# An expert's two weights in one transfer, and the queries' left-over rows behind the odd batches' rows

## The chip, the cores and the metric

The kernel runs on one core of one Trainium2 chip. What is counted is the device time of one execution, in microseconds (us). The core has a matrix engine (TensorE, PE in the profile), a vector engine (DVE), a scalar engine (ACT), GpSimd (POOL) and SyncE (SP). SP issues nearly all transfers from memory here and does nothing else; its transfers form one queue that 16 DMA engines work off. A tile has 128 partitions, and one row of a transfer is what goes to one partition.

## The reference

Three stages, all in float32, on 8 batches of 576 tokens (4608 tokens), 8 heads of 64:

```python
# slot attention
a = softmax(phi, over the 576 tokens)            # 32 memory slots per head
k_m, v_m = a^T k, a^T v                          # 32 x 64 per head
x = softmax(q k_m^T / 8, over the slots) v_m     # 4608 x 512
# soft mixture of 8 experts with 4 slots each
logits = x phi                                   # 4608 x 32
slot_input = softmax(logits, over the tokens)^T x        # 8 experts x 4 rows x 512
slot_out[e] = relu(slot_input[e] w1[e]) w2[e]    # w1: 512 x 1024, w2: 1024 x 512
x = softmax(logits, over the slots) slot_out     # 4608 x 512
# MLP
out = softplus(x w_in) w_out                     # 512 -> 2048 -> 512
```

An expert works on four rows only, so its two matrices of 2 MB each are used by few and short matmuls. The experts' weights are 33.6 of the 85.0 MB that the kernel reads.

## The kernel before, in words

**Stages.** The attention goes through the batches in order. Of each batch it loads `phi`, `kv` and `q`; the 576 tokens are 512 and 64 left over, and the left-over rows of two batches are scored together. Then the dispatch softmax gives the experts' inputs, the experts run, and their outputs are folded with the first MLP matrix; the MLP takes the rest.

**Who decides the order.** The program is written by a planner, `Flow` (lines 149 to 275). Each step of the kernel is a generator that yields units: a list of (engine, estimated us) and the tokens and slots that the unit needs. `Flow` starts the unit that can start earliest by these estimates, so the order of instructions on each engine follows from the estimated durations of the loads too. `keep_warm` puts idle matmuls (line 938) where the planner's own times show gaps on PE.

**Loads.** All loads are issued by SP in one order: first `attention_loads` (line 428), which per batch yields kv, the next batch's phi, q, and with an odd batch `qm`, the left-over rows of two batches. Then `weight_loads` (line 1086): four MLP transfers, the experts' weights `w` (`load_w1`, line 1036, and `load_w2`, line 1044) in the order w1 of expert 0, w2 of expert 0, and so on to expert 5, then w1 of 6 and 7, w2 of 6 and 7, and then the other `wi` and `wo` of the MLP. The last w2 comes in parts of 1, 0.5 and 0.5 MB. An instruction on SP that waits holds up those behind it.

**Room.** Each load needs a free slot of a ring or pool. `q` has a ring of 3 slots of 8 KB per partition, `qm` one of 2 slots of 2 KB; a slot is free when the scores (`raw_scores`, line 568, matmul in line 591) that read it are done. The experts' weights have 8 slots of 16 KB (`w16`, line 1013), which lie where the attention had its buffers; a slot is given back in line 1259 after an expert's first layer, or in line 1296 after its second.

**The experts on PE.** `first_layer` (line 1244) computes `hid` with w1 (matmul in line 1251), ACT applies relu (`hs`), PE transposes (`hTp`, line 1267), ACT copies it to `hT`. `second_layer` (line 1275) adds every expert's product of `hT` and w2 into `S` (line 1284). After the last expert's, `slot_out` sums up the parts (`sop`, line 1308). Between them stand transposes `ctp` (line 1221) of the combine weights `c` (line 1215).

Of the kernel before, what the change touches and what calls it, by code (L numbers as in the profile page):

```python
# [134 lines left out]

    "left": 52000,

    "rings": (("kv", 3), ("phi", 3), ("a", 4), ("kt", 6), ("s", 2), ("q", 3), ("qm", 2)),

    "stick": 'm1 n2 n3 r3 t1',  # L140
}
# [7 lines left out]
class Flow:  # L149
# [50 lines left out]
    def free(self, name, i=0):  # L200
        self.pools[name].append((*self.now, i))
# [77 lines left out]
def tile_slot_attention_soft_moe_softplus_mlp(  # L279
    ctx: ExitStack,  # L280
    tc: tile.TileContext,
    q: bass.AP,
    qm: bass.AP,
    kv: bass.AP,
    phi: bass.AP,
    moe_phi: bass.AP,
    moe_w1: bass.AP,
    moe_w2: bass.AP,
    w_in: bass.AP,
    w_out: bass.AP,  # L290
    out: bass.AP,
# [50 lines left out]
    def weight_pools(stack, name, some):  # L342
# [12 lines left out]
    A_ORDER = (2, 3, 0, 1)  # L355
    sizes = {
        "kv": 2 * KV + KVL, "phi": NG * S, "kt": 256, "s": (SC + 1) * 2 * TM, "a": (SC + 1) * 2 * TM,
        "q": 4 * 128 * SC, "qm": 4 * 128,
    }
    for tag, n in PLAN["rings"]:  # L360
        pools = B1 if tag in ("kv", "phi") else BB
# [49 lines left out]
                done(f"kv{b}{g}")  # L411

    def load_q(b):
        yield [("D", 2.52)], ["+q"], 0
        t, held["q", b] = ring("q")
        nc.sync.dma_start(out=t, in_=q[b])
        q_t[b] = t.rearrange("p (k n) -> p k n", k=4)
        done(f"q{b}")
        if b % 2 == 0:
            return  # L420
        pr = b // 2
        yield [("D", 0.63)], ["+qm"], 0
        t, held["qm", pr] = ring("qm")
        nc.sync.dma_start(out=t, in_=qm[pr])
        qm_t[pr] = t.rearrange("p (k b n) -> p k b n", k=4, b=2)
        done(f"qm{pr}")

    def attention_loads():
        yield from load_phi(0)
# [138 lines left out]
    def raw_scores(b, half):  # L568


        pr, bb = divmod(b, 2)
        yield [("P", 0.3 if half else 0.95)], (
            [f"qm{pr}", f"km{b}0", f"km{b}1", f"sr{b}"] if half
            else [f"q{b}", f"km{b}0", f"km{b}1", "+a"]
        ) + ["+raw"]
        if not half:
            a, held["a", b] = ring("a")
            raw_t[b] = a
            a_t[b] = a.rearrange("p (c x) -> p c x", c=SC + 1)
# [19 lines left out]
        if half:  # L599
            free("qm", held["qm", pr])  # L600
        else:
            free("q", held["q", b])
# [407 lines left out]
    pp = px.enter_context(tc.tile_pool(name="pp", bufs=1, reuse_waits="tile", space=PSUM))  # L1010
    ex = px.enter_context(tc.tile_pool(name="ex", bufs=1, reuse_waits="tile"))
    w8.update(weight_pools(ctx, "w8", range(NWS, NW1)))
    w16 = weight_pools(px, "w16", range(NW1 // 2, (NW8 + NWX) // 2))
    vacant = [
        max([t for x, y, t in taken if x < edge - 8192 * i and y > edge - 8192 * (i + 1)], default=0.0)
        for i in range(NW8 + NWX)
    ]
    flow.pools["w8"] = [(vacant[i], "", i) for i in w8]
    flow.pools["w16"] = [(max(vacant[2 * i : 2 * i + 2]), "", i) for i in w16]

    def slot8(shape, dtype, name, i=None):

# [5 lines left out]

    w1_t, w2_t, raw_t, at = {}, {}, {}, {}

    def slot16():

        i = flow.got["w16"]
        return i, w16[i].tile([128, 4096], F32, tag="w16", name="w16")

    def load_w1(e):
        yield [("D", 4.93)], ["+w16"], 0
        at["w1", e], t = slot16()
        nc.sync.dma_start(out=t, in_=moe_w1[e])
        for n in range(2):  # L1040
            w1_t[e, n] = t[:, 2048 * n : 2048 * n + 2048].rearrange("p (k f) -> p k f", k=KC)
        done(f"w1{e}")

    def load_w2(e):
        last = e == NE - 1
        parts = ((0, 2048), (2048, 3072), (3072, 4096)) if last else ((0, 4096),)
        for a, b in parts:
            yield [("D", 4.93 * (b - a) / 4096)], [] if a else ["+w16"], 0
            if a == 0:
                at["w2", e], t = slot16()  # L1050
                for n in range(2):
                    w2_t[e, n] = t[:, 2048 * n : 2048 * n + 2048].rearrange("p (h k d) -> p h k d", h=2, k=4)
            nc.sync.dma_start(out=t[:, a:b], in_=moe_w2[e][:, a:b])
            for n in range(2):
                for half in range(2):
                    if a <= 2048 * n + 1024 * half < b:
                        done(f"w2{e}{n}.{half}")
# [28 lines left out]
    def weight_loads():  # L1086
        early = list(EARLY)
        for _ in range(early_at.count(-1)):
            x = early.pop(0)
            yield from load_wi(x[1]) if x[0] == "wi" else load_wo(x[1])  # L1090
        for e in range(NE):
            for x in (e, e + 1) if e == NE - 2 else (e,) if e < NE - 2 else ():
                yield from load_w1(x)
            yield from load_w2(e)
            for _ in range(early_at.count(e)):
                x = early.pop(0)
                yield from load_wi(x[1]) if x[0] == "wi" else load_wo(x[1])
# [146 lines left out]
    def first_layer(e):  # L1244
        yield [("P", 2.0)], ["SX", f"w1{e}", "+hid"]
        if e == NE - 1:
            flow.product = product
        hid = pp.tile([128, 256], F32, tag="hid", bufs=2, name="hid")
        for kc in range(KC):
            for j in range(4):  # L1250
                nc.tensor.matmul(  # L1251
                    hid[32 * j : 32 * j + 32],
                    lhsT=SX[:, kc, NS * e : NS * e + NS],
                    rhs=w1_t[e, j // 2][:, kc, 256 * (j % 2) : 256 * (j % 2) + 256],
                    start=(kc == 0),
                    stop=(kc == KC - 1),
                    skip_group_check=True,
                )
        free("w16", at["w1", e])
        yield [("A", 0.39)], []  # L1260
        hs = ex.tile([128, 256], F32, tag="hs", bufs=2, name="hs")
        nc.scalar.activation(hs, hid, AF.Relu)
        free("hid")
        yield [("P", 0.22)], ["+hTp"]
        hTp = pp.tile([128, 2, 128], F32, tag="hT", name="hTp")
        for cb in range(2):
            nc.tensor.transpose(hTp[:, cb], hs[:, 128 * cb : 128 * cb + 128], ident)
        yield [("A", 0.39)], ["+hT"]
        hT = ex.tile([128, 2, 4, NS], F32, tag="hTs", bufs=2, name="hT")
        nc.scalar.activation(hT.rearrange("p c j s -> p c (j s)"), hTp, AF.Copy)  # L1270
        free("hTp")
        hT_t[e] = hT
        done(f"hT{e}")

    def second_layer():
        for n in range(2 * NE):
# [16 lines left out]
                    done(f"s2{half}")  # L1293
                    flow.add(slot_out(half), -1e5 + half, "ex")
            if kb:
                free("w16", at["w2", e])
                free("hT")

    def slot_out(half):
# [56 lines left out]
    flow.AFTER = Flow.AFTER  # L1356
    px.close()
    w8.update(weight_pools(ctx, "w8", range(NW1, NW8)))
    flow.pools["w8"] += [(t, e, n) for t, e, i in flow.pools["w16"] for n in (2 * i, 2 * i + 1) if n < NW8]
# [517 lines left out]
    n = 0  # L1877
# [68 lines left out]
def _laid_out(q, k, v, phi, moe_phi, moe_w1, moe_w2, moe2_w_in, moe2_w_out):  # L1946
# [9 lines left out]
    qt = qt[:, :, :, :full].reshape(b, 128, -1)  # L1956
# [51 lines left out]
```

## Time and profile before

| what | us |
|---|---|
| median of 3 runs | 570.96 (570.64 to 571.28) |
| the profiled execution | 570.84 |
| its span, first to last instruction | 569.1 |
| PE busy | 542.0 (95%) |
| DVE busy | 462.2 (81%) |
| ACT busy | 374.7 (66%) |
| SP's queue (q1 in the profile): 96.81 MB | 41.9% of 16 engines' span |

The mean granted clock of TensorE was 0.994 of full speed. Between the profiled execution and its span lie 1.7 us in which no instruction is shown. The profile cuts the span into 40 slices of 14.2 us. In the first 13 the DMA engines are busy throughout, later they aren't; PE is at eight or nine tenths in nearly all slices. A transfer is shown twice: by its issue on SP, with the start of the issue, and by the time from issue to landing. Lines such as L1284 are lines of the kernel before.

### The profile page before, as it was taken

To read this page: it belongs to the slowest core of one execution; us is meant where nothing else is said; L and a number is where in the kernel's file an instruction comes from. 1 tells how busy PE (TensorE), PEld (TensorE's weight loads), DVE (VectorE), ACT (ScalarE), POOL (GpSimd) and SP (SyncE) were. 2 spreads that over 40 slices of the span, in tenths; PEclk is the share of its full clock that TensorE was granted. 3 is DMA by queue.
4 is the path that set the end of the run, shared out by engine and by line. 5 is a ranking of instruction groups with operands and counts; after the bars stand their busy time and mean duration, and the time that the engine had idled before them with its cause. 6 is when DMAs were issued, how large, how long until landed. Compare 5 with 4: busy or idle time off the path is not lost.

```text
span 569.1 us, 10050 instructions
## 1 busy us (share of the span) xinstructions
PE 542.0 (95%) x4043; PEld 415.3 (73%) x4050; DVE 462.2 (81%) x605; ACT 374.7 (66%) x530; POOL 61.1 (11%) x76
## 2 busy tenths in 40 slices
PE   8888989999589999999999999999999999999997
PEld 4566656545346888888888888888888888888885
DVE  3788888988805998999999999999999758778953
ACT  3767766434413898588967976887887976765520
POOL 1000000000000001001023121221112110211100
PEclk9999999999979999999999999999999999999999
DMA  9999999999999476558598876899658554765832
GB/s 363 420 411 425 416 420 424 426 426 423 423 420 409 187 221 151 194 158 184 219 230 152 158 118 105 151 152 184 103 97 156 94 85 73 122 113 115 164 80 111
DMA packets 24671, 132.06 MB, mean 232 GB/s; under 512 B 3248, under 2 KB 4912, under 8 KB 18352
## 3 DMA queue, kind: packets, MB, share of 16 engines
q1 hardware_dynamic: 15120, 96.81, 41.9%
q0 software_dynamic: 9504, 34.61, 35.2%
q8 instruction: 32, 0.52, 0.4%
q14 instruction: 15, 0.12, 0.1%
HBM read 85.00 MB, written 42.47 MB: 224 GB/s over the span
## 4 chain that ended last, share of the span: by engine, by line
PE 84%; DMA 8%; DVE 5%; ACT 2%; issue 1%; POOL 0%; DVEq 0%; ACTq 0%; POOLq 0%
PE ob L1803 53%; DMA w<-in_moe_w_dram 8%; PE ob L1657 8%; PE hp L1684 5%; PE idle L938 3%; PE kvp L511 3%; PE rp L591 1%; PE tp L694 1%; PE sc L630 1%; PE tp L466 1%; PE ob L1831 1%; PE U L841 1%; ACT a L610 1%; PE kvp L534 1%; PE hid L1251 1%; PE hp L1573 1%
## 5 line engine op out<-in xcount | busy, mean ns | idle before, releaser
L1803 PE MATMUL ob<-g,WS 128*128 128x512 f32 x768 | 181.8, 389 | 0.0
L1803 PEld LDWEIGHTS ob<-g,WS 128*128 128x128 f32 x768 | 144.0, 188 | 30.2 <-issue 0.4
L1803 PE MATMUL ob<-g,W 128*128 128x512 f32 x552 | 130.5, 389 | 0.0
L1803 PEld LDWEIGHTS ob<-g,W 128*128 128x128 f32 x552 | 103.6, 188 | 21.7 <-ACT outs L819 0.2
L819 ACT ACTIVATE outs<-ob 128x1024 f32<-128x1024 f32 x78 | 80.1, 1027 | 52.8 <-PE ob L1803 42.2
L1445 POOL DMA_DIRECT2D out_dram<-outs x60 | 53.1, 919 | 453.3 <-DMA out_dram<-outs 228.5
L1750 DVE TENSOR_TENSOR g<-arena,g 128x1024 fp32r<-128x1024 f32 x61 | 74.1, 1220 | 19.6 <-ACT g L1748 19.5
L1748 ACT ACTIVATE g<-arena 128x1024 fp32r<-128x1024 f32 x61 | 64.2, 1056 | 16.3 <-PE ob L1803 13.4
L1657 PE MATMUL ob<-g,W 128*128 128x512 f32 x192 | 46.5, 390 | 0.0
L1438 DVE TENSOR_TENSOR outs<-ob,outs 128x1024 f32<-128x1024 f32 x30 | 36.7, 1223 | 11.2 <-PE ob L1803 9.8
L1657 PEld LDWEIGHTS ob<-g,W 128*128 128x128 f32 x192 | 36.0, 188 | 7.5
L1684 PE MATMUL hp<-CT,Gs 128*128 128x512 f32 x128 | 38.5, 390 | 0.0
L1750 DVE TENSOR_TENSOR g<-x,g 128x1024 fp32r<-128x1024 f32 x26 | 31.4, 1220 | 3.2 <-ACT g L1748 3.1
L1750 DVE TENSOR_TENSOR g<-room,g 128x1024 fp32r<-128x1024 f32 x25 | 30.1, 1220 | 2.0 <-ACT g L1748 2.0
L1748 ACT ACTIVATE g<-x 128x1024 fp32r<-128x1024 f32 x26 | 27.5, 1057 | 4.4 <-PE ob L1803 2.3
L1748 ACT ACTIVATE g<-room 128x1024 fp32r<-128x1024 f32 x25 | 26.3, 1057 | 5.1 <-PE ob L1803 4.4
L1697 ACT ACTIVATE arena<-hp 128x1024 f32<-128x1024 f32 x30 | 29.6, 1017 | 0.0
L938 PE MATMUL idle<-zero 128*128 128x512 bf16 x100 | 26.8, 402 | 2.4 <-POOL zero L941 1.5
L1684 PEld LDWEIGHTS hp<-CT,Gs 128*128 128x128 f32 x128 | 24.0, 188 | 5.1 <-issue 0.2
L1284 PE MATMUL S<-w,hT 128*32 128x256 f32 x256 | 17.5, 413 | 3.8 <-ACT hT L1270 2.6
L511 PE MATMUL kvp<-kv,et 128*32 128x128 f32 x512 | 18.2, 276 | 1.2 <-ACT vp L554 0.9
L938 PEld LDWEIGHTS <-zero 128*128 128x128 bf16 x107 | 10.2, 102 | 12.5 <-issue 3.9
(204 smaller groups left out, 727.7 us busy)
## 6 DMA issues: line engine op xcount, KB each, us to landing
w<-in_moe_w_dram SPq DMA_DIRECT2D x15, 2048.0 KB, 21.7
out_dram<-outs POOLq DMA_DIRECT2D x60, 512.0 KB, 5.2
kv<-in_kv_dram SPq DMA_DIRECT2D x7, 2304.0 KB, 25.0
out_dram<-outs SPq DMA_DIRECT2D x20, 512.0 KB, 2.9
q<-in_q_dram SPq DMA_DIRECT2D x8, 1024.0 KB, 21.4
wi<-in_w_in_dram SPq DMA_DIRECT2D x8, 1024.0 KB, 17.9
wo<-in_w_out_dram SPq DMA_DIRECT2D x8, 1024.0 KB, 15.9
phi<-in_phi_dram SPq DMA_DIRECT2D x8, 576.0 KB, 19.8
```

Of the source, the lines that this page charges most:

```text
L511: nc.tensor.matmul(kvp[32 * h : 32 * h + 32], lhsT=rows[:, 32 * h : 32 * h + 32], rhs=rows_of[:, c, h] if c < SC else rest[:, h], start=(c ...
L819: nc.scalar.activation(o, i, AF.Copy)
L938: nc.tensor.matmul(idle[0], lhsT=zero[:, :128], rhs=zero, start=True, stop=True)
L1284: nc.tensor.matmul(S2[half][32 * i : 32 * i + 32], lhsT=hT_t[e][:, kc8 % 2, kc8 // 2], rhs=w2_t[e, kb][:, half, i], start=(n == 0), stop=( ...
L1438: nc.vector.tensor_tensor(out=o, in0=OB[at], in1=o, op=ALU.add)
L1445: nc.gpsimd.dma_start(out=place(half, tb), in_=o, accum_op=ALU.add)
L1657: nc.tensor.matmul(bank(oc), lhsT=W[u][:, w, i, c], rhs=hb[tb, u][:, x, i], start=(fresh and i == chunks[0] and k == "0"), stop=(stop and ...
L1684: nc.tensor.matmul(hp[:, i], lhsT=Gs[:, 128 * fc : 128 * fc + 128], rhs=CTf[:, TB * tb : TB * tb + TB], start=True, stop=True,)
L1697: nc.scalar.activation(X[key][:, m], hp, AF.Softplus)
L1748: nc.scalar.activation(g[:, 0], x, AF.Copy)
L1750: nc.vector.tensor_tensor(out=g[:, 1], in0=x, in1=g.bitcast(F32)[:, 0], op=ALU.subtract)
L1803: nc.tensor.matmul(OB[at][:, t], lhsT=(W if w == "W" else WS)[u][:, x, c, cols], rhs=g[:, y, m], start=(fresh and u == grp[0] and n == 0), ...
```

## The change

The tensor of the left-over query rows is gone. Its rows stand behind the q rows: a row of q has 10 KB now, of which an even batch's transfer reads the first 8 KB and an odd batch's all 10 KB. The slots of the q ring have 10 KB, the ring `qm` is gone, and an odd batch's slot is given back when both its scores and the left-over scores have read it.

The experts' 16 matrices lie as 8 pairs in one tensor with rows of 32 KB: w1 and w2 of experts 0 to 4, then w1 of 5 and 6, w1 of 7 with w2 of 5, and w2 of 6 and 7. Pairs 0 to 6 are one transfer of 4 MB each; the last comes in parts of 2, 1, 0.5 and 0.5 MB. Instead of 8 slots of 16 KB there are 4 of 32 KB in the same place, and a slot is given back when both halves have been used.

```diff
     def load_q(b):
-        yield [("D", 2.52)], ["+q"], 0
+
+        n, m = 4 * 128 * SC, 4 * 128
+        end = n + m * (b % 2)
+        yield [("D", 2.52 + 0.58 * (b % 2))], ["+q"], 0
         t, held["q", b] = ring("q")
-        nc.sync.dma_start(out=t, in_=q[b])
-        q_t[b] = t.rearrange("p (k n) -> p k n", k=4)
+        nc.sync.dma_start(out=t[:, :end], in_=q[b][:, :end])
+        q_t[b] = t[:, :n].rearrange("p (k n) -> p k n", k=4)
         done(f"q{b}")
-        if b % 2 == 0:
-            return
-        pr = b // 2
-        yield [("D", 0.63)], ["+qm"], 0
-        t, held["qm", pr] = ring("qm")
-        nc.sync.dma_start(out=t, in_=qm[pr])
-        qm_t[pr] = t.rearrange("p (k b n) -> p k b n", k=4, b=2)
-        done(f"qm{pr}")
+        if b % 2:
+            qm_t[b // 2] = t[:, n:].rearrange("p (k b n) -> p k b n", k=4, b=2)
+            done(f"qm{b // 2}")
+            rows_of_q[b] = 2
+
+    def leave_q(b):
+        rows_of_q[b] = rows_of_q.get(b, 1) - 1
+        if rows_of_q[b] == 0:
+            free("q", held["q", b])
...
-    w16 = weight_pools(px, "w16", range(NW1 // 2, (NW8 + NWX) // 2))
+    w32 = weight_pools(px, "w32", range(NW1 // 4, (NW8 + NWX) // 4))
...
-    def load_w1(e):
-        yield [("D", 4.93)], ["+w16"], 0
-        at["w1", e], t = slot16()
-        nc.sync.dma_start(out=t, in_=moe_w1[e])
...
+    def expert_loads():
+
+        order = [x for e in range(NE - 3) for x in (("w1", e), ("w2", e))]
+        order += [("w1", NE - 3), ("w1", NE - 2), ("w1", NE - 1)]
+        order += [("w2", NE - 3), ("w2", NE - 2), ("w2", NE - 1)]
+        for n in range(NE):
+            pair = order[2 * n : 2 * n + 2]
+            ends = [0, 8192] if n < NE - 1 else [0, 4096, *(4096 + y for _, y in LAST_PARTS)]
+            for a, b in zip(ends, ends[1:]):
+                yield [("D", 0.03 + 9.7 * (b - a) / 8192)], [] if a else ["+w32"], 0
+                if a == 0:
+                    i = flow.got["w32"]
+                    both = w32[i].tile([128, 8192], F32, tag="w32", name="w")
+                    for k, (kind, e) in enumerate(pair):
+                        at[kind, e] = i
+                        views(kind, e, both[:, 4096 * k : 4096 * k + 4096])
+                nc.sync.dma_start(out=both[:, a:b], in_=moe_w[n][:, a:b])
+                for k, (kind, e) in enumerate(pair):
+                    arrived_w(kind, e, a - 4096 * k, b - 4096 * k)
+
+    in_w = defaultdict(lambda: 2)
+
+    def leave_w(i):
+        in_w[i] -= 1
+        if in_w[i] == 0:
+            in_w[i] = 2
+            free("w32", i)
+
+    LAST_PARTS = ((0, 2048), (2048, 3072), (3072, 4096))
...
+    def arrived_w(kind, e, a, b):
+        if kind == "w1":
+            done(f"w1{e}")
+            return
+        for n in range(2):
+            for half in range(2):
+                if a <= 2048 * n + 1024 * half < b:
+                    done(f"w2{e}{n}.{half}")
...
-        free("w16", at["w1", e])
+        leave_w(at["w1", e])
...
-                free("w16", at["w2", e])
+                leave_w(at["w2", e])
...
+    mw = np.concatenate(
+        [np.stack([w1, w2], axis=1).reshape(2 * e, 128, -1)[: 2 * e - 6], w1[e - 3 :], w2[e - 3 :]]
+    ).reshape(e, 2, 128, -1).transpose(0, 2, 1, 3).reshape(e, 128, -1)
```

The last three lines are in `_laid_out`, which only brings the inputs into the order in memory. Where the instructions stand, before and after, at three places:

On SP, the end of the attention's loads and the first MLP loads, before. In brackets are the semaphores that an instruction waits for.

```order
L416 DMA q<-in_q_dram 128x2048 [waits DMAHW2_49,PE_49]
L409 DMA kv<-in_kv_dram 128x4608 [waits DMAHW3_49,PE_49]
L416 DMA q<-in_q_dram 128x2048 [waits DMAHW4_49,PE_49]
L424 DMA qm<-in_qm_dram 128x512 [waits DMAHW5_49]
L1078 DMA wi<-in_w_in_dram 128x2048 [waits DMAHW6_49]
L1069 DMA wo<-in_w_out_dram 128x2048 [waits DMAHW7_49]
```

The same place with the change:

```order
L417 DMA q<-in_q_dram 128x2048 [waits DMAHW7_49,PE_49]
L407 DMA kv<-in_kv_dram 128x4608 [waits DMAHW0_49,PE_49]
L417 DMA q<-in_q_dram 128x2560 [waits DMAHW1_49,PE_49]
L1101 DMA wi<-in_w_in_dram 128x2048 [waits DMAHW2_49]
L1092 DMA wo<-in_w_out_dram 128x2048 [waits DMAHW3_49]
```

One transfer has gone, and the last q has 2560 values per partition instead of 2048; the waits for PE stand where they stood.

On SP, the experts' weights that follow, before. w_1953 and w_1955 are w1 and w2 of expert 0, w_1957 and w_1959 those of expert 1, and so on to w_2204 and w_2243 of expert 5.

```order
L1039 DMA w_1953<-in_moe_w_dram 128x4096 [waits DMAHW2_49,DVE_49,PE_49]
L1053 DMA w_1955<-in_moe_w_dram 128x4096 [waits DMAHW3_49,PE_49]
L1039 DMA w_1957<-in_moe_w_dram 128x4096 [waits DMAHW4_49]
L1053 DMA w_1959<-in_moe_w_dram 128x4096 [waits DMAHW5_49,PE_49]
L1039 DMA w_1961<-in_moe_w_dram 128x4096 [waits DMAHW6_49,PE_49]
L1053 DMA w_1963<-in_moe_w_dram 128x4096 [waits DVE_49,DMAHW7_49,Activation_49,Pool_49]
L1039 DMA w_1986<-in_moe_w_dram 128x4096 [waits DVE_49,DMAHW0_49,PE_49,Activation_49]
L1053 DMA w_2047<-in_moe_w_dram 128x4096 [waits DMAHW1_49,DVE_49,Activation_49]
L1039 DMA w_2106<-in_moe_w_dram 128x4096 [waits DMAHW2_49,PE_49]
L1053 DMA w_2147<-in_moe_w_dram 128x4096 [waits DMAHW4_49,DMAHW3_49,PE_49]
L1039 DMA w_2204<-in_moe_w_dram 128x4096 [waits DMAHW6_49,PE_49]
L1053 DMA w_2243<-in_moe_w_dram 128x4096 [waits DMAHW5_49,PE_49]
```

With the change, the seven pairs and the first two parts of the last:

```order
L1051 DMA w<-in_moe_w_dram 128x8192 [waits DMAHW6_49,DMAHW0_49,PE_49]
L1051 DMA w<-in_moe_w_dram 128x8192 [waits DMAHW7_49,DMAHW1_49,PE_49]
L1051 DMA w<-in_moe_w_dram 128x8192 [waits DVE_49,Activation_49,Pool_49]
L1051 DMA w<-in_moe_w_dram 128x8192 [waits DVE_49,PE_49,Activation_49]
L1051 DMA w<-in_moe_w_dram 128x8192 [waits DMAHW6_49,DMAHW2_49,PE_49]
L1051 DMA w<-in_moe_w_dram 128x8192 [waits DMAHW7_49,DMAHW3_49,PE_49]
L1051 DMA w<-in_moe_w_dram 128x8192 [waits DMAHW4_49,DMAHW0_49,PE_49]
L1051 DMA w<-in_moe_w_dram 128x4096 [waits DMAHW5_49,DMAHW1_49,PE_49]
L1051 DMA w<-in_moe_w_dram 128x2048
```

Twelve transfers of 4096 values per partition before are six pairs of 8192 now. The pair in the first row carries the wait for PE that the second transfer had, and the pair in the fifth row the one that the twelfth had.

On PE, the end of the experts' stage before. w_2204 is w1 of expert 5, w_2243 its w2, w_2296 and w_2325 are w1 of experts 6 and 7.

```order
L1251 MATMUL hid<-w_2204,room 32x256 x16
L1221 MATMUL ctp<-ident,c_2274 128x128 x4
L1267 MATMUL hTp<-ident,hs 128x128 x2
L1221 MATMUL ctp<-ident,c_2308 128x128 x4
L1284 MATMUL S_1942<-w_2243,hT 32x256 x4
L1284 MATMUL S_1943<-w_2243,hT 32x256 x4
L1284 MATMUL S_1942<-w_2243,hT 32x256 x4
L1284 MATMUL S_1943<-w_2243,hT 32x256 x4
L1251 MATMUL hid<-w_2296,room 32x256 x16
L1267 MATMUL hTp<-ident,hs 128x128 x2
L1251 MATMUL hid<-w_2325,room 32x256 x16
```

The same place with the change; the first S row is the end of expert 4's second layer, and hid is that of experts 5 and 6, then of 7:

```order
L1301 MATMUL S_1919<-w,hT 32x256 x4
L1238 MATMUL ctp<-ident,c_2245 128x128 x4
L1268 MATMUL hid<-w,room 32x256 x32
L1284 MATMUL hTp<-ident,hs 128x128 x4
L1301 MATMUL S_1918<-w,hT 32x256 x4
L1301 MATMUL S_1919<-w,hT 32x256 x4
L1301 MATMUL S_1918<-w,hT 32x256 x4
L1301 MATMUL S_1919<-w,hT 32x256 x4
L1268 MATMUL hid<-w,room 32x256 x16
```

Expert 5's second layer has moved from between the first layers of 5 and 6 to behind both; the combine transposes `ctp` stand ahead of them. The idle matmuls before expert 6's second layer are 8 now and were 12.

## Rows read from the trace of the kernel before

**Rows 1.** The page's chain that ended last: its shares of the span by line.

```profile
PE ob L1803 53%; DMA w<-in_moe_w_dram 8%; PE ob L1657 8%; PE hp L1684 5%; PE idle L938 3%; PE kvp L511 3%; PE rp L591 1%; PE tp L694 1%; PE sc L630 1%; PE tp L466 1%; PE ob L1831 1%; PE U L841 1%; ACT a L610 1%; PE kvp L534 1%; PE hid L1251 1%; PE hp L1573 1%
```

**Rows 2.** The chain of waits in 118 to 180 us: start us, us, what.

```profile
126.55 17.09 DMA w<-in_moe_w_dram
...
143.66 30.66 DMA w<-in_moe_w_dram
...
174.36 0.64 PE S L1284 x8
```

**Rows 3.** Busy time by stretch: length, PE, PEld, DVE, ACT, POOL, PEclk, DMA, GB/s.

```profile
150.00:155.00 5.00, 1.64 (x18) 0.68 (x10) 4.07 (x7) 2.22 (x4) 0.00 (x0) 1.00 0.99 419
155.00:160.00 5.00, 2.91 (x24) 1.60 (x28) 2.26 (x4) 1.93 (x3) 0.00 (x0) 0.56 0.99 423
160.00:165.00 5.00, 4.49 (x58) 2.06 (x54) 0.00 (x0) 0.41 (x2) 0.00 (x0) 0.76 0.99 419
...
176.00:560.00 384.00, 384.00 (x1790) 317.52 (x1789) 332.35 (x332) 282.80 (x310) 58.48 (x66) 1.00 0.68 149
```

**Rows 4.** The page's 40 slices of 14.2 us: DMA busy, in tenths.

```profile
DMA  9999999999999476558598876899658554765832
```

**Rows 5.** Timeline of SP's queue: start us, us, engine, line, transfer.

```profile
63.85 0.42 SPq L424 DMA_DIRECT2D qm<-in_qm_dram  x1
64.33 0.42 SPq L1078 DMA_DIRECT2D wi<-in_w_in_dram  x1
...
92.03 0.33 SPq L1053 DMA_DIRECT2D w<-in_moe_w_dram  x1
...
131.13 0.33 SPq L1053 DMA_DIRECT2D w<-in_moe_w_dram  x1
...
135.53 0.33 SPq L1039 DMA_DIRECT2D w<-in_moe_w_dram  x1
139.31 4.67 SPq L1053 DMA_DIRECT2D w<-in_moe_w_dram  x4
...
228.14 0.34 SPq L1078 DMA_DIRECT2D wi<-in_w_in_dram  x1
```

**Rows 6.** The same transfers but 131.13's, issue to landing: count, KB, us.

```profile
qm<-in_qm_dram SPq DMA_DIRECT2D x1, 256.0 KB, 20.3
wi<-in_w_in_dram SPq DMA_DIRECT2D x1, 1024.0 KB, 22.3
...
w<-in_moe_w_dram SPq DMA_DIRECT2D x1, 2048.0 KB, 12.3
...
w<-in_moe_w_dram SPq DMA_DIRECT2D x1, 2048.0 KB, 27.6
w<-in_moe_w_dram SPq DMA_DIRECT2D x1, 2048.0 KB, 30.0
...
wi<-in_w_in_dram SPq DMA_DIRECT2D x1, 1024.0 KB, 4.7
```

**Rows 7.** Timeline of PE in the experts' stage: start us, us, line, operation.

```profile
129.16 1.91 PE L1284 MATMUL S<-w,hT 128*32 128x256 f32 x32
...
158.20 3.64 PE L1284 MATMUL S<-w,hT 128*32 128x256 f32 x32 [0.96 <-ACT hT L1270]
161.62 2.30 PE L1251 MATMUL hid<-w,room 128*32 128x256 f32 x32
...
164.81 1.93 PE L1251 MATMUL hid<-w,room 128*32 128x256 f32 x32
166.90 1.67 PE L938 MATMUL idle<-zero 128*128 128x512 bf16 x7 [0.16 <-issue]
168.41 0.38 PE L1267 MATMUL hTp<-ident,hs 128*128 128x128 f32 x2
...
169.58 1.93 PE L1284 MATMUL S<-w,hT 128*32 128x256 f32 x32
171.91 1.81 PE L1284 MATMUL S<-w,hT 128*32 128x256 f32 x24 [0.40 <-DMA w<-in_moe_w_dram]
```

More of the change, by code (lines that the diff above doesn't have):

```diff
@@ L136 @@
     "left": 52000,
-    "rings": (("kv", 3), ("phi", 3), ("a", 4), ("kt", 6), ("s", 2), ("q", 3), ("qm", 2)),
+    "rings": (("kv", 3), ("phi", 3), ("a", 4), ("kt", 6), ("s", 2), ("q", 3)),
     "stick": 'm1 n2 n3 r3 t1',
@@ L282, in tile_slot_attention_soft_moe_softplus_mlp @@
     q: bass.AP,
-    qm: bass.AP,
     kv: bass.AP,
@@ L286, in tile_slot_attention_soft_moe_softplus_mlp @@
     moe_phi: bass.AP,
-    moe_w1: bass.AP,
-    moe_w2: bass.AP,
+    moe_w: bass.AP,
     w_in: bass.AP,
@@ L357, in tile_slot_attention_soft_moe_softplus_mlp @@
         "kv": 2 * KV + KVL, "phi": NG * S, "kt": 256, "s": (SC + 1) * 2 * TM, "a": (SC + 1) * 2 * TM,
-        "q": 4 * 128 * SC, "qm": 4 * 128,
+        "q": 4 * 128 * (SC + 1),
     }
@@ L413, in load_q @@
     def load_q(b):
-        yield [("D", 2.52)], ["+q"], 0
+        n, m = 4 * 128 * SC, 4 * 128
+        end = n + m * (b % 2)
+        yield [("D", 2.52 + 0.58 * (b % 2))], ["+q"], 0
         t, held["q", b] = ring("q")
-        nc.sync.dma_start(out=t, in_=q[b])
-        q_t[b] = t.rearrange("p (k n) -> p k n", k=4)
+        nc.sync.dma_start(out=t[:, :end], in_=q[b][:, :end])
+        q_t[b] = t[:, :n].rearrange("p (k n) -> p k n", k=4)
         done(f"q{b}")
-        if b % 2 == 0:
-            return
-        pr = b // 2
-        yield [("D", 0.63)], ["+qm"], 0
-        t, held["qm", pr] = ring("qm")
-        nc.sync.dma_start(out=t, in_=qm[pr])
-        qm_t[pr] = t.rearrange("p (k b n) -> p k b n", k=4, b=2)
-        done(f"qm{pr}")
+        if b % 2:
+            qm_t[b // 2] = t[:, n:].rearrange("p (k b n) -> p k b n", k=4, b=2)
+            done(f"qm{b // 2}")
+            rows_of_q[b] = 2
+    rows_of_q = {}
+    def leave_q(b):
+        rows_of_q[b] = rows_of_q.get(b, 1) - 1
+        if rows_of_q[b] == 0:
+            free("q", held["q", b])
     def attention_loads():
@@ L599, in raw_scores @@
         if half:
-            free("qm", held["qm", pr])
+            leave_q(2 * pr + 1)
         else:
-            free("q", held["q", b])
+            leave_q(b)
         if half:
@@ L1018, in tile_slot_attention_soft_moe_softplus_mlp @@
     flow.pools["w8"] = [(vacant[i], "", i) for i in w8]
-    flow.pools["w16"] = [(max(vacant[2 * i : 2 * i + 2]), "", i) for i in w16]
+    flow.pools["w32"] = [(max(vacant[4 * i : 4 * i + 4]), "", i) for i in w32]
     def slot8(shape, dtype, name, i=None):
@@ L1029, in tile_slot_attention_soft_moe_softplus_mlp @@
     w1_t, w2_t, raw_t, at = {}, {}, {}, {}
-    def slot16():
-        i = flow.got["w16"]
-        return i, w16[i].tile([128, 4096], F32, tag="w16", name="w16")
-    def load_w1(e):
-        yield [("D", 4.93)], ["+w16"], 0
-        at["w1", e], t = slot16()
-        nc.sync.dma_start(out=t, in_=moe_w1[e])
-        for n in range(2):
[L1041 to L1057, printed above, removed]
+    def expert_loads():
[16 more added lines that the diff above has]
+                    arrived_w(kind, e, a - 4096 * k, b - 4096 * k)
@@ new lines, in tile_slot_attention_soft_moe_softplus_mlp, with views @@
+    in_w = defaultdict(lambda: 2)
[5 more added lines that the diff above has]
+    LAST_PARTS = ((0, 2048), (2048, 3072), (3072, 4096))
+    def views(kind, e, t):
+        if kind == "w1":
+            for n in range(2):
+                w1_t[e, n] = t[:, 2048 * n : 2048 * n + 2048].rearrange("p (k f) -> p k f", k=KC)
+            return
+        for n in range(2):
+            w2_t[e, n] = t[:, 2048 * n : 2048 * n + 2048].rearrange("p (h k d) -> p h k d", h=2, k=4)
@@ L1059, in tile_slot_attention_soft_moe_softplus_mlp @@
+    def arrived_w(kind, e, a, b):
+        if kind == "w1":
+            done(f"w1{e}")
+            return
+        for n in range(2):
+            for half in range(2):
+                if a <= 2048 * n + 1024 * half < b:
+                    done(f"w2{e}{n}.{half}")
     wi_v = w_in.bitcast(I32)
@@ L1090, in weight_loads @@
             yield from load_wi(x[1]) if x[0] == "wi" else load_wo(x[1])
[L1091 to L1097, printed above, removed]
+        yield from expert_loads()
         for x in early + LATE:
@@ L1358, in tile_slot_attention_soft_moe_softplus_mlp @@
     w8.update(weight_pools(ctx, "w8", range(NW1, NW8)))
-    flow.pools["w8"] += [(t, e, n) for t, e, i in flow.pools["w16"] for n in (2 * i, 2 * i + 1) if n < NW8]
+    flow.pools["w8"] += [(t, e, n) for t, e, i in flow.pools["w32"] for n in range(4 * i, 4 * i + 4) if n < NW8]
     pb = ctx.enter_context(tc.tile_pool(name="pb", bufs=1, reuse_waits="tile", space=PSUM))
@@ L1955, in _laid_out @@
     qm = qt[:, :, :, full:].reshape(b // 2, 2, 128, 4, s - full).transpose(0, 2, 3, 1, 4).reshape(b // 2, 128, -1)
-    qt = qt[:, :, :, :full].reshape(b, 128, -1)
+    qt = np.concatenate([qt[:, :, :, :full].reshape(b, 128, -1), np.repeat(qm, 2, axis=0)], axis=2)
     pt = phi.reshape(b, 2, 4, s, m).transpose(0, 2, 4, 1, 3).reshape(b, 128, 2, s)
@@ L1971, in _laid_out @@
     wo = moe2_w_out.reshape(ff // 256, 2, 128, dm).transpose(0, 2, 1, 3).reshape(ff // 256, 128, -1)
-    return {"q": qt, "qm": qm, "kv": kvt, "phi": pt, "moe_phi": mp, "moe_w1": w1, "moe_w2": w2, "w_in": wi, "w_out": wo}
+    return {"q": qt, "kv": kvt, "phi": pt, "moe_phi": mp, "moe_w": mw, "w_in": wi, "w_out": wo}
 def _in_order(o):
```

## The prediction

> **What bounds the kernel now.** I read the chain of work that ended last first. PE holds 84% of it, most in the MLP's second product, and one transfer kind holds 8%: `w<-in_moe_w_dram`, the experts' weights [rows 1]. So there are two regimes, and the table by stretches places them: from 176 to 560 us PE is busy 384.00 of 384.00 us [rows 3]. Whatever happens to loads in there is hidden, and whatever moves the start of this block moves the end by the same amount. The chain cut to the time before it shows what sets that start: two long pieces of weight transfer one after the other, the second ending at 143.66 + 30.66 = 174.32, and 0.04 later the last eight matmuls of expert 7's second layer [rows 2]. The weights come over SP's one queue, and the DMA row of the slices shows it at nine tenths or more from the start for 13 slices of 14.2 us, 185 us [rows 4]. Until 174 us the kernel is thus bound by bytes in one queue: a change counts there only if it makes the queue's row of transfers end at another time.
>
> **What a transfer costs in a full queue.** In a full queue I take the distance between two landings, not issue to landing. The left-over rows qm are issued at 63.85 and land 20.3 later, at 84.15; the wi behind them is issued at 64.33 and lands 22.3 later, at 86.63 [rows 5, 6]. So 1 MB in rows of 8 KB takes 2.48 us, or 4.96 for two such transfers. Expert 0's second weight lands at 92.03 + 12.3 = 104.33 and expert 7's first, twelve transfers of 2 MB (rows of 16 KB) later, at 135.53 + 27.6 = 163.13: 58.80 / 12 = 4.90 each. The same bytes in one transfer with rows of twice the length are 0.06 us cheaper than in two. The landings are given to 0.1, so the figure for one wi can be 0.1 off: from both sides 0 to 0.12 per merger. I take 0.06, the difference of the rows; that it is the same from 16 to 32 KB as from 8 to 16 KB is my assumption.
>
> **The queries' left-over rows.** Four qm transfers go, and their 2 KB per partition stand at the end of the odd batches' q rows, with the same bytes. 4 x 0.06 = 0.24 us leave the queue; bounds 0 and 0.48. The even batches read 8 KB out of each 10 KB, rows of the same length as before. The q slot of an odd batch is now free only after the left-over scores. With a ring of three, a q is issued while some 20 us of work lie ahead of it in the queue (q and qm at 63 to 64 us land 20 us later), so a slot that is free a few us later starves nothing: 0.
>
> **The experts' weights.** Of 18 transfers, 11 remain: 14 matrices of 2 MB go as 7 pairs of 4 MB, and the last two stay cut as 2, 1, 0.5 and 0.5 MB. Seven mergers at 0.06 are 0.42 us; bounds 0 and 0.84.
>
> **What the pairs wait for.** A pair's slot is free only when both halves are. Pair 0 may be issued when the second transfer was, at 92.03, where the first had gone earlier. Its data begin some 2.2 us after the issue: a lone wi, at 228.14, lands after 4.7, of which 2.48 are its bytes [rows 5, 6]. 92.03 + 2.2 + 2 x 4.90 - 0.06 = 103.97; by the queue alone it lands at 104.33 - 0.24 - 0.06 = 104.03. The issue is just early enough. Pair 4 waits for the end of expert 0's second layer on PE, 129.16 + 1.91 = 131.07 [rows 7], where expert 5's second weight was issued at 131.13; its second half had gone at 126.55. By the issue it lands at 131.13 + 2.2 + 9.74 = 143.07; by the queue at 126.55 + 17.09 = 143.64 [rows 2], less 0.24 and five mergers, 143.10. Both are even to 0.1, so I cost the two waits at 0. They can be up to 0.4 late together (if the first byte takes 2.4 under load) and cannot gain, since the queue was never empty there. The later pairs wait for the second layers of experts 1 to 3, with two or three pairs still ahead of them in the queue. What stands behind a waiting pair on SP is only the following pairs and the late wi and wo, and PE is never out of work in the block that uses those.
>
> **TensorE.** Expert 5's second weight now comes with expert 7's first instead of two places ahead. Expert 5's second layer moves behind the first layers of 5 and 6, and eight idle matmuls stand before expert 6's second layer instead of twelve. Pair 6 lands at 163.13 - 0.66 = 162.47, and the second layer starts 0.27 later, as expert 6's does after its landing (139.31 + 30.0 = 169.31, start 169.58). At the full clock it takes 1.93 to 164.67, expert 7's first layer 1.93 to 166.60 (it ended at 164.81 + 1.93 = 166.74 before), eight idle matmuls at 1.67 / 7 = 0.24 each to 168.51, the transposes 0.38 to 168.89. Expert 6's second weight lands at 169.31 - 0.66 = 168.65. So this work is hidden by that landing, with 168.65 + 0.27 = 168.92 as the start. Cost 0. Cover: the last eight matmuls start at 174.36 - 0.66 = 173.70, and 1.93 + 1.81 are due before them, so expert 6's second layer may start as late as 169.96, 1.04 later.
>
> **The sum.** -0.24 - 0.42 + 0 + 0 = -0.66. The profiled execution took 570.84 us (its span 569.1 and 1.7 around it), so 570.18; the median of the runs is 0.12 above it: 570.3.
>
> **A rule against it.** The weights' rows lie 32 KB apart in memory now, 16 KB before. From 8 to 16 KB the trace shows no loss, 4.96 against 4.90 for 2 MB [rows 5, 6]. The Trainium skill, "DMA: Bandwidth & Descriptors", section "Latency and other measured facts", says that pitches of large powers of two slow copies from HBM, with 207 GB/s at 512 KB a row, 164 at 2 MB, and 214 once padded. As an estimate from that page, even 512 KB would cost 3%, and the sum would be 572.4. No run of before shows 32 KB; it is a rival below.
>
> **Rivals.**
> 1. *The clock comes late* (slower). In 155 to 160 us the granted clock is 0.56 and in 160 to 165 it is 0.76, so it stood at the lower of its two levels (1.2 of 2.4 GHz) for much of both, after 150 to 155 in which PE was busy 1.64 of 5 us [rows 3]; expert 5's second layer took 3.64 and the first layer behind it 2.30 [rows 7]. Now PE has little between the first layers of 5 and 6 (from about 153 to 157) and pair 6 at 162.5, nearly 6 us. If the low level falls on the work behind pair 6: 162.74 + 3.64 + 2.30 + 1.91 + 0.38 = 170.97, which is 1.01 past the cover: 570.3 + 1.0 = 571.3. If the first layer also takes twice 1.93, 1.56 more, 572.9. Middle 572.1. It decides as soon as more than 1.04 of delay comes together. Against it: PE works from 153 to 157 where it did nothing, and the stall must last through nearly the whole second layer. 0.20.
> 2. *Nothing comes of the rows.* The longer rows cost the same per byte, or one of the waits eats the gain: 570.9 to 571.1. For it: 0.06 is at the grain of the landings. 0.08.
> 3. *The saving is twice as large*, as the bounds allow: -0.48 - 0.84 = -1.32, 569.6. 0.10.
> 4. *Rows 32 KB apart are fetched more slowly.* Each per cent of pace is 14 x 4.90 / 100 = 0.69 us; from 1% on it eats the gain, at 3% it makes 570.3 + 2.1 = 572.4. Against it the two paces above. 0.04.
> 5. *Every transfer pays a fixed price of its own in the queue*, and the change takes 4 + 7 of them away. Two wi of 1 MB against one weight of 2 MB bound it: 0.06, not a whole first-byte time; if it were the 2.2 us of a lone transfer, 11 x 2.2 = 24 us would go, 546. The rows speak plainly against it: 0.01. The Trainium skill, "DMA: Bandwidth & Descriptors", section "Anatomy of one DMA — SWDGE (gpsimd) path", gives a transfer 2.0 us and its bytes at 436 GB/s, for another issue path; 4.90 from landing to landing for 2 MB holds no such 2.0 us.
>
> **How the numbers follow.** The forecast, 570.3, has 0.57, with its own range of 569.6 to 570.9 from the bounds of rows and waits. The range 569.4 to 572.1 takes in rivals 2 and 3 and the lower half of the clock's, and leaves out about 0.16: half of rival 1, rivals 4 and 5. A measurement of this kernel tells 0.2%, 1.14 us, from no change, so faster is below 569.82 and slower above 572.10. Faster: rival 3, rival 5 and a fifth of the forecast, 0.23. Slower: half of rival 1 and most of 4, 0.14. Same: the rest, 0.63.
>
> **What would show it.** The row of 4 MB landings should be 9.74 apart, pair 4 should land near 143.1 and the last part near 173.7, and from there to the end nothing should change. Landings more than 9.80 apart would show that the rows save nothing; a gap in the DMA share around 92 or 131 us would show a wait that costs; a first layer of expert 7 ending after 168 us, with the granted clock at 0.5 behind 162, would show rival 1. If PE's block after 176 us gets idle time, or the time before 85 us changes by more than half a microsecond, the reading itself was wrong.

## The result, and the profile after

The changed kernel takes 574.14 us (median of 15 runs, 571.93 to 576.47), the kernel before 570.96. The ratio is 1.0055, with a 95% interval of 1.0040 to 1.0071: slower by 2.3 to 4.1 us, where 570.3 was forecast. The runs, which lay within 0.7 us of each other before, are now 4.5 us apart. The profiled execution took 574.35, its span is 572.6, 3.5 longer than before.

The MLP is as it was. PE is full in it, for 383.00 of 383.00 us now (384.00 before), so again it is the experts' end that moved. All of the following is the changed kernel. First the busy times by stretch, with the columns of [rows 3]:

```profile
91.00:95.00 4.00, 4.00 (x86) 3.15 (x78) 3.38 (x9) 1.70 (x4) 0.00 (x0) 1.00 0.14 53
95.00:97.00 2.00, 2.00 (x30) 1.30 (x34) 1.90 (x6) 1.70 (x6) 0.00 (x0) 1.00 0.96 270
...
134.00:137.00 3.00, 1.95 (x35) 0.94 (x32) 2.93 (x5) 1.18 (x3) 0.00 (x0) 1.00 0.85 306
...
165.00:170.00 5.00, 2.31 (x24) 1.17 (x28) 0.00 (x0) 0.00 (x0) 0.00 (x0) 0.73 0.94 401
...
180.00:563.00 383.00, 383.00 (x1785) 316.76 (x1785) 331.57 (x331) 282.74 (x309) 58.52 (x66) 1.00 0.69 150
```

The last two columns are the ones to read. From 91 to 95 us the DMA engines moved 53 GB/s, from 95 to 97 270 and from 134 to 137 306, where a full queue moves some 424. In bytes at that pace, (424 - 53) x 4 + (424 - 270) x 2 is 4.2 us of queue lost, and 0.8 more behind 134. The kernel before has 434, 410 and 426 in the same stretches; two of its rows:

```profile
91.00:95.00 4.00, 4.00 (x86) 2.48 (x78) 3.86 (x10) 2.72 (x7) 0.00 (x0) 1.00 1.03 434
...
134.00:137.00 3.00, 2.27 (x34) 1.28 (x26) 2.90 (x4) 1.16 (x4) 0.00 (x0) 1.00 1.00 426
```

The two places are those where the prediction had put the two waits at 0.

The issues on SP, and what the transfers took from issue to landing (columns as in [rows 5, 6]):

```profile
94.38 0.33 SPq L1051 DMA_DIRECT2D w<-in_moe_w_dram  x1
...
133.47 0.33 SPq L1051 DMA_DIRECT2D w<-in_moe_w_dram  x1
```

```profile
wo<-in_w_out_dram SPq DMA_DIRECT2D x1, 1024.0 KB, 22.2
...
w<-in_moe_w_dram SPq DMA_DIRECT2D x1, 4096.0 KB, 12.7
...
w<-in_moe_w_dram SPq DMA_DIRECT2D x1, 4096.0 KB, 14.7
...
w<-in_moe_w_dram SPq DMA_DIRECT2D x1, 2048.0 KB, 26.7
```

The wo ahead of the experts was issued at 71.42 and landed at 93.62. Pair 0 was issued at 94.38, 0.8 behind that landing, and landed at 107.08 (104.33 before, 104.03 forecast). Pair 4, issued at 133.47, landed at 148.17 (143.64 before, 143.10 forecast). Expert 6's second weight, the 2 MB at the end, was issued at 145.82 and landed at 172.52 (169.31 before).

The chain of waits, which answers to [rows 2]:

```profile
141.66 25.99 DMA w<-in_moe_w_dram
167.65 0.04 issue
167.69 3.42 PE S L1301 x32
171.12 1.73 PE hid L1268 x32
172.84 1.83 PE idle L942 x8
174.68 0.22 PE hTp L1284 x2
174.89 3.20 PE S L1301 x56
```

It no longer ends with the last landing and eight matmuls. It runs from pair 6, landing at 167.66, through PE's work behind it: expert 5's second layer at the lower clock (3.42 instead of 1.93), the first layer of 7, eight idle matmuls. PE was late here by a little: from the landing at 172.52 the end of the S matmuls would have come 3.21 after that of before, at 174.36 + 3.21 + 0.64 = 178.21, and they ended at 178.48 (174.82 and 3.66 on PE's timeline). So 3.2 of the 3.5 us are transfers, 0.3 the clock.

Why pair 0 was issued at 94.38 and not at 92.03 shows on PE. Batch 7's last kvp, on which it waits:

```profile
93.02 1.08 PE L515 MATMUL kvp<-kv,et 128*32 128x128 f32 x32
93.91 0.40 PE L515 MATMUL kvp<-kv,er 128*32 128x128 f32 x8
```

It ended at 94.31; before, it ended at 91.96:

```profile
91.56 0.40 PE L511 MATMUL kvp<-kv,er 128*32 128x128 f32 x8
```

The attention's matmuls are the same. But TensorE's clock stood at 0.66 in 78 to 83 us of this execution (1.00 before):

```profile
78.00:83.00 5.00, 5.00 (x70) 4.36 (x73) 2.62 (x5) 2.54 (x7) 0.00 (x0) 0.66 0.98 406
```

PE had been busy 2.07 of the 3 us ahead of them, and 2.19 in the trace before, where no fall followed. It was busy throughout these 5 us, so the clock took some 0.34 x 5 = 1.7 us of the 2.35. The other 0.7 had been lost before: batch 7's kv, which waits for PE, was issued at 60.67 and not at 59.95.

### The profile page after: what moved, and what is told of

Same layout as the page of the kernel before. It is cut to its first block, busy times and chain, and to the rows that moved or that the text cites. A ratio compares the mean times of both kernels' runs of the same rounds, so it can differ in the third digit from the quotient of the medians.

```text
span 572.6 us, 10019 instructions
## 1 busy us (share of the span) xinstructions
PE 544.2 (95%) x4046; PEld 416.7 (73%) x4046; DVE 462.2 (81%) x605; ACT 374.7 (65%) x530; POOL 61.2 (11%) x76
## 4 chain that ended last, share of the span: by engine, by line
PE 87%; DVE 5%; DMA 5%; ACT 2%; issue 1%; POOL 0%; ACTq 0%; DVEq 0%; POOLq 0%
PE ob L1820 52%; PE ob L1674 8%; PE hp L1701 5%; DMA w<-in_moe_w_dram 5%; PE idle L942 3%; PE kvp L515 3%; PE S L1301 2%; PE hid L1268 2%; PE sc L634 1%; PE rp L595 1%; PE tp L698 1%; PE tp L470 1%; PE ob L1848 1%; PE U L845 1%; ACT a L614 1%; PE hp L1590 1%
## 5 line engine op out<-in xcount | busy, mean ns | idle before, releaser
L942 PE MATMUL idle<-zero 128*128 128x512 bf16 x103 | 28.1, 411 | 1.5 <-POOL zero L945 1.5
L639 DVE TENSOR_REDUCE smx<-sc 128x16 f32<-128x512 f32 (+1 forms) x20 | 12.6, 630 | 9.5 <-PE sc L634 9.5
L1301 PEld LDWEIGHTS S<-w,hT 128*32 128x32 f32 x256 | 8.7, 124 | 14.7 <-DMA w<-in_moe_w_dram 5.0
```

Of the source, the lines that this page charges most:

```text
L942: nc.tensor.matmul(idle[0], lhsT=zero[:, :128], rhs=zero, start=True, stop=True)
L1301: nc.tensor.matmul(S2[half][32 * i : 32 * i + 32], lhsT=hT_t[e][:, kc8 % 2, kc8 // 2], rhs=w2_t[e, kb][:, half, i], start=(n == 0), stop=( ...
```

## The experiments

**The queries' part alone.** The kernel before with the new `load_q`, its ring and `leave_q`; the experts' transfers as before.

```diff
-    "rings": (..., ("q", 3), ("qm", 2)),
+    "rings": (..., ("q", 3)),
...
-        nc.sync.dma_start(out=t, in_=q[b])
+        nc.sync.dma_start(out=t[:, :end], in_=q[b][:, :end])
```

> Only the queries' part of the change: qm rows behind the odd batches' q rows; the experts' weights stay 18 transfers of 2 MB and less with 8 slots. Theory of the dry queue (the pairs are issued after the queue has run empty, around 91 to 97 and 134 to 137 us; rows and sizes cost nothing): the queue is never empty here, four transfers fewer end it 0.2 to 1.0 earlier, 570.0 to 570.8, runs as close together as those of before. Rival, the queries' merger disturbs the attention (its matmuls were 0.75 late from 12 us and met the lower clock at 79 to 82): 571.5 to 574 with wide runs. Rival, size (4 MB transfers and rows of 32 KB are slow by themselves): like the first.

570.74 (570.12 to 572.28) against 571.09 for the kernel before, measured beside it, ratio 0.9994 (0.9985 to 1.0003): 0.35 less, not clear of zero, and of the size of the 0.24. The upper end of the range is in the profile: this execution had the clock low in 26 to 34 us and its attention ended at 94.56, yet its first expert transfer had been issued at 79.28 and the queue stayed full. Its last weight landed at 145.44 + 28.8 = 174.24, no later than before. That it still took 572.28 lies on PE: late from the attention on, with the clock at 0.65, 0.50 and 0.82 in the three stretches of 155 to 170 us, it ended the S matmuls at 176.70, where they ended at 175.00 before. Three of the runs of the kernel before took as long (572.46 to 572.55). No cost of the queries' merger shows.

**Pairs in two halves.** The changed kernel with each pair as two transfers of 2 MB into the same slots.

```diff
-            ends = [0, 8192] if n < NE - 1 else [0, 4096, ...]
+            ends = [0, 4096, 8192] if n < NE - 1 else [0, 4096, ...]
```

> The changed kernel, but each of the seven pairs goes as two transfers of 2 MB (16 KB of each row, rows still 32 KB apart in memory) into the same slots of 32 KB, issued one behind the other. Theory of the dry queue: the waits stay, so the loss stays, 573 to 576 with wide runs, the queue empty around 92 and 134 us. Rival, size: without rows of 32 KB in one transfer the time comes back to 570.3 to 571.0.

573.98 (571.10 to 575.32), ratio 1.0044 (1.0027 to 1.0060): the loss of the changed kernel, without any transfer of 4 MB. So the size of a transfer is not the cause. The slots, the rows 32 KB apart and the order on PE are still those of the changed kernel here.

**The first wait alone.** The kernel before, with the first transfer sent to the slot that the second had.

```diff
-        yield [("D", 4.93)], ["+w16"], 0
+        yield [("D", 4.93)], ["+w16" + PICK.get(("w1", e), "")], 0
...
+    PICK = {("w1", 0): "=2", ("w2", 0): "=3", ("w1", 1): "=4"}
```

> The kernel before with one thing changed: the first expert transfer goes into the slot that the second had, and the second into the third's, so that the first waits for the end of batch 7's last kvp as pair 0 does. Sizes, rows and the number of transfers stay as before. Theory of the dry queue: the first weight is issued at about 92 instead of 85.2, after the bytes ahead of it have gone out, and lands late by 0.4 to 1.5: 571.4 to 572.5, and the runs spread by more than 1 us, since the attention's end on PE now sets the queue. Rival, size: 570.96.

571.28 (570.79 to 573.85), ratio 1.0017 (1.0004 to 1.0031); the median lies just below the range that I expected. The runs stand in two groups, seven from 570.79 to 571.47 and four from 573.28 to 573.85. The profile is of the first group: the attention ended at 91.64, the first weight was issued at 91.70, and 91 to 95 us moved 244 GB/s. So the wait alone makes a gap even when the attention is early, but in this execution the gap cost no time: the first weight landed 1.1 later than before (100.5 for 99.4), expert 6's second weight at 169.2, as before. The second group was not profiled.

**The second wait alone.** The kernel before, with expert 4's first weight sent to the slot of expert 0's second.

```diff
+    PICK = {("w1", 4): "=2"}
...
```

> The kernel before with one thing changed: expert 4's first weight goes into the slot of expert 0's second weight, so that it is issued only after expert 0's second layer (131.1 instead of 124.1), as pair 4 is. Sizes and rows as before. Theory of the dry queue: at 131.1 most engines have little left to do, the landing of expert 4's second weight goes from 143.65 to 144 to 145.5, time 571.2 to 572.5. Rival (my prediction's working): even to 0.1, 570.9 to 571.1.

572.74 (570.74 to 573.81), ratio 1.0025 (1.0012 to 1.0038); the median lies just above the range that I expected. The runs lie near 570.8, 571.9 and 573.6. The profile is of the third group, with the late attention (its last kvp ended at 94.55); the other two were not profiled. Its stretches before and at the wait:

```profile
91.00:95.00 4.00, 4.00 (x90) 3.39 (x86) 3.48 (x9) 1.50 (x3) 0.00 (x0) 1.00 1.04 434
...
131.00:134.00 3.00, 3.00 (x56) 1.73 (x47) 2.93 (x5) 0.93 (x4) 0.00 (x0) 1.00 0.22 87
134.00:137.00 3.00, 3.00 (x53) 1.81 (x55) 2.90 (x6) 1.56 (x4) 0.00 (x0) 1.00 0.79 213
```

The weight ahead of the waiting one and the waiting one itself, issue to landing:

```profile
w<-in_moe_w_dram SPq DMA_DIRECT2D x1, 2048.0 KB, 22.5
...
w<-in_moe_w_dram SPq DMA_DIRECT2D x1, 2048.0 KB, 8.4
```

These two answers are the core of the case. The weight ahead (issued at 111.11) landed at 133.61. But the 16 engines together were busy only 0.22 of 131 to 134 us, so most of them had nothing left some two us before that landing. Cut more finely, their share is 0.94 from 128 to 131 us, 0.37 from 131 to 132.75, and 0.00 from there to 134.5. So no byte moved in the last 0.9 us before the landing, nor in the first 0.8 behind the next issue. And the waiting weight, issued at 133.72, took 8.4 to land where 4.90 is its share in a full queue: a restart costs 3.5, not the 2.2 that I had taken.

**Both waits, nothing else.** The kernel before with both edits.

```diff
+    PICK = {("w1", 0): "=2", ("w2", 0): "=3", ("w1", 1): "=4", ("w1", 4): "=3"}
...
```

> The kernel before with both late issues of the two runs before this and nothing else: the first expert transfer waits for the end of batch 7's last kvp, expert 4's first weight for the end of expert 0's second layer; 18 transfers of 2 MB and less, qm apart. Theory of the dry queue: the two waits alone make the loss of the changed kernel, 572.7 to 574.5, with runs spread over 3 us or more. Rival, something else in the change costs besides the waits: near 572.7, what the later of the two waits made alone, or less.

573.87 (571.72 to 574.05), ratio 1.0042 (1.0030 to 1.0055). With no pair and no merger the two late issues make 2.4 us, most of the 1.0055 of the changed kernel. The run at 571.72 is the profiled one: its attention ended early, at 91.60, and its last weight landed at 175.3, 1.0 later than before. The other four, from 573.61 to 574.05, I take for executions with the late end; none of them was profiled. With the one wait or the other the last group lies near 573.6, so the two waits do not seem to add up when the attention is late. The group at 576 is missing, and the runs spread over 2.3, not over the 3 that I expected.

**The pairs alone.** The changed kernel with the qm transfers of before.

```diff
-    "rings": (..., ("q", 3)),
+    "rings": (..., ("q", 3), ("qm", 2)),
```

> Only the experts' part of the change: pairs of 4 MB in slots of 32 KB, with the qm transfers as before. Theory of the dry queue: like the changed kernel, 573 to 575.5, perhaps 0.3 less than it, since the queue in front of the first pair is 0.24 longer. Rival, the queries' merger has a part in the loss: 571.5 to 572.5.

574.41 (572.09 to 576.73), ratio 1.0073 (1.0057 to 1.0089). All of the loss is in the experts' part. The profiled run, at 572.09, had the early end (91.57), and its last weight landed at 175.3 too.

**Pairs without the two waits.** The changed kernel with five pairs grouped anew and four matrices alone, so that the first weight and expert 4's first weight have slots of their own; the last transfers stay single.

```diff
+    GROUPS = [
+        ("w16", 4, 0, 0, [("w1", 0)]),
+        ("w32", 1, 1, 0, [("w2", 0), ("w1", 1)]),
+        ("w32", 3, 2, 0, [("w2", 1), ("w1", 2)]),
+        ("w16", 5, 0, 1, [("w2", 2)]),
+        ("w32", 4, 3, 0, [("w1", 3), ("w2", 3)]),
+        ("w16", 4, 6, 0, [("w1", 4)]),
+        ("w32", 1, 4, 0, [("w2", 4), ("w1", 5)]),
+        ("w32", 3, 5, 0, [("w2", 5), ("w1", 6)]),
...
```

> The changed kernel, but the two transfers that found the queue empty are single matrices again, in slots of their own of 16 KB: expert 0's first weight goes ahead alone (slot vacant as before, issue at about 85) and expert 4's first weight alone into expert 0's slot (issue after expert 0's first layer, about 124 to 127). Five pairs of 4 MB with rows of 32 KB stay, grouped anew, and the queries' merger stays. Theory of the dry queue: the queue is never empty before 174 us, the loss is gone, and what is left is 0.24 for the queries and 5 x 0.06 for the pairs: 570.2 to 570.9, the runs as close as those of the queries' part alone (570.1 to 572.3). Rival, size or pitch of the 4 MB transfers: most of the loss stays, 572 or more.

570.05 (569.65 to 570.23), ratio 0.9983 (0.9975 to 0.9992) against 570.85 before: faster than both kernels, a little below the range that I expected, and the closest runs of all. In its profile:

```profile
91.00:95.00 4.00, 4.00 (x92) 3.37 (x86) 3.39 (x9) 1.50 (x3) 0.00 (x0) 1.00 1.00 416
95.00:97.00 2.00, 2.00 (x26) 1.12 (x18) 1.90 (x6) 1.69 (x5) 0.00 (x0) 1.00 1.08 410
...
131.00:134.00 3.00, 3.00 (x56) 1.73 (x46) 2.93 (x5) 0.93 (x3) 0.00 (x0) 1.00 1.01 426
```

The queue is full in both places, although this execution had the late attention (its last kvp ended at 94.53). The two weights were issued at 87.77 and 126.68. Around the second place the landings follow at full pace, 133.5, 138.4 and 148.1, with 2 MB and then 4 MB between them. With the waits gone the loss is gone, and a saving is left.

**Idle matmuls ahead of expert 5's second layer.**

```diff
+                if (e, kb, half) == (NE - 3, 0, 0):
+                    for _ in range(14):
+                        product()
```

> The changed kernel with 14 more idle matmuls on PE ahead of expert 5's second layer, where PE stands still for some 5 us until pair 6 lands and the clock has fallen to 0.5 in the profile. First rival of the prediction (the low clock behind pair 6 sets the end): the second layer takes 1.93 again instead of 3.42 and the time falls by 0.7 to 1.5 against the changed kernel on the same chip. Theory of the dry queue: the last parts of expert 7's second weight land about 177.5 whatever PE does before, so the time stays within 0.4.

**The changed kernel again, beside it.** Unaltered but for a comment.

```diff
+# again
```

> The changed kernel unaltered, as the measure for the run with idle matmuls, and for a second profile of it. Both theories: 572 to 576.5, median about 574. If the attention's end on PE sets the spread, the profile shows batch 7's last kvp near 91.6 with a time below 573.1, near 94.3 with one between 573.9 and 574.9, and something later or a second empty stretch with one above 575.8.

With idle matmuls 571.95 (571.54 to 574.85, 11 runs), unaltered 576.20 (575.38 to 576.53, 4 runs); the ratios to the kernel before, 571.17 here, are 1.0023 (1.0009 to 1.0036) and 1.0087 (1.0073 to 1.0101). The difference is more than either theory gave, and not one effect. The profile of the first, at 571.95, has the attention's end at 91.90, and the times and mean granted clocks of its runs fit nine of eleven without a fall in the attention. The profile of the second, at 576.53, ended it at 94.39. So some 2.5 us of the difference are the attention, which the edit does not touch. Why so many runs were early with the edit and none of the four without it stays open. The rest is on PE in the second:

```profile
168.58 3.64 PE L1301 MATMUL S<-w,hT 128*32 128x256 f32 x32 [4.64 <-DMA w<-in_moe_w_dram]
171.99 3.04 PE L1268 MATMUL hid<-w,room 128*32 128x256 f32 x32
...
177.02 3.66 PE L1301 MATMUL S<-w,hT 128*32 128x256 f32 x64
```

The last part of the weights, issued at 147.27, took 31.2 and landed at 178.47. The S matmuls could have ended 0.64 later, at 179.11, and they ended at 180.68: here the low clock cost 1.6. With the idle matmuls the same layer took 1.93 and the first layer behind it 1.91. My expectation that the clock costs nothing was wrong. In this run near 576 the late attention and the low clock come together, and I read the other runs near 576 in the same way; the two longest runs with idle matmuls, 574.45 and 574.85, fit the late attention alone.

## Why the prediction was wrong

**What bounds the kernel** was read rightly: the MLP is full, the weights' queue sets its start, and of the 4.5 us that pair 6 was late 3.2 reached the end.

**The rows' saving** (0.24 and 0.06 a merger) agrees with the runs, which do not measure it more closely. For the kernel with five pairs and the queries' merger it gives 0.24 + 5 x 0.06 = 0.54; measured 0.97, from 0.5 to 1.4. Single landings are no measure for it: the wo ahead of the experts, with the same queue in front of it, landed at 94.57 in the trace before, 94.15 and 93.88 in the two runs with one wait.

**What the pairs wait for** is the step that failed. "The issue is just early enough" and "both are even to 0.1, so I cost the two waits at 0" stood on a comparison of landings, with 0.4 as the worst. Both waits alone cost 2.4 (1.7 to 3.1), in a mix of one early and four longer executions. Three things were wrong in it.

- A landing is not the end of the queue's work. Most engines ran dry some two us earlier (0.22 busy in the three us around the landing at 133.61), and the last packet had moved 0.9 before it. The Trainium skill, "DMA: Bandwidth & Descriptors", section "Why a DMA increments its semaphore by 16 and not by 1", says that the engines of a transfer finish independently and that only the full count means that all data is there; the trace of the second wait agrees, with 0.37 busy in 131 to 132.75 us.
- The restart was priced by a lone transfer of 1 MB, 4.7 - 2.48 = 2.2, read as the time until "its data begin". In the trace that transfer's engines stand still for the first 0.96 us and the last 0.64, and the bytes between take 3.10: the data begin after 1.0. After a dry queue pair 0 took 12.7 - 9.74 = 3.0 beyond its bytes, 13.5 - 9.74 = 3.8 in the second profile of the changed kernel, the waiting weight 8.4 - 4.90 = 3.5, and the first half of pair 0 in the run with halves 8.9 - 4.90 = 4.0.
- The end of the attention, 91.96, and of expert 0's second layer, 131.07, were taken from one execution as if they were fixed. They are some 2.4 us later when the clock falls in the attention (0.62 in 25 to 34 us or 0.66 in 78 to 83). The transfers of the kernel before, at 85.21 and 124.1, leave 7 us of cushion for that, and the run with five pairs lost nothing by it: 570.23 with the late attention. A coupled slot spends exactly this cushion. With both waits and the early end the last weight landed 1.0 to 1.1 later than before (175.3 to 175.4 for 174.32, three profiles), with one wait or both and the late end 2.8 to 4.2 later (177.1 to 178.5, four profiles).

What I wrote down as "even to 0.1" was thus a landing 2.75 late for pair 0 (107.08 for 104.33) and 4.5 late for pair 4 (148.17 for 143.64) in the profile of the changed kernel.

**TensorE.** Expert 5's second layer did go behind pair 6, and the clock did fall on it, as the first rival said: 3.42 and 3.64 for 1.93. I had given this 0.20 and it came in both profiles of the changed kernel. The price was 0.3 in one and 1.6 in the other, on either side of the rival's 1.0. The cover of 1.04 was sized too small: the 1.81 us of the 24 matmuls [rows 7] hold a wait for a landing, and the 56 matmuls ahead of the last eight take 3.20 in one go in the chain above, not 1.93 + 1.81 = 3.74. That makes some 1.6. The low clock adds to the loss but is not its main cause: both waits with expert 5's layers in their old place make 573.87.

**Rows 32 KB apart** cost nothing: five pairs of them make 570.05. So the rule that I weighed, of the Trainium skill, "DMA: Bandwidth & Descriptors", section "Latency and other measured facts", shows no effect at this pitch; no run here shows the larger pitches that it speaks of.

**Open.** In the profiled execution pair 6 is 4.5 late, but the next weight only 3.2: before, 6.18 us lie between the landings at 163.13 and 169.31 for 2 MB, now 4.86. The queue did not stand still there before: it is 0.99 busy up to 165 us [rows 3], and in 163 to 169 us 100 of the 256 rows of 4 KB of the last two parts had moved already, ahead of the landing at 169.31; now none had in 166 to 172. So before, some engines were ahead of those that this landing waited for. That the dry stretches have set them even again is my reading, not shown. Nor is it settled why the clock falls in the attention in most runs of one program and in few of another, though the attention's matmuls are the same.

## What to carry to other kernels

A merged transfer starts when the later of its two rooms is free, and the earlier start was worth more here (2.4 us) than a longer row (0.06). Before costing such a wait at nothing, look at when the DMA engines run dry, not at when the last transfer lands, add the restart, and ask how far the awaited instruction moves from run to run. Here the engines ran dry two us before the landing, the first byte came 0.8 behind the issue and the awaited end moved by 2.4: as an estimate from these, a margin below 5 us in one trace was none. Merge those whose rooms come free together and leave alone the few at which the queue is short.

## What the runs showed of the hardware that I had not expected

With the same matmuls the attention ended near 91.7 or near 94.4, according to whether the granted clock fell to the lower of its two levels at one of two places: 0.62 over 25 to 34 us with PE late by 2.6 from there on, or 0.66 over 78 to 83, with 0.7 to 1.0 lost earlier. All eleven profiles follow this, five early and six late; the one of the kernel before is early, and its own late executions are not shown. And the queue's restart after a dry stretch took 3.0 to 4.0 us beyond the bytes, against 2.2 for one lone transfer of 1 MB.
